# Linear attention and an MLP on one core: batch 1's loads moved to the software queue, chunks 1, 2 and 9 begun in token halves

## The chip, the core and the metric

The kernel runs on one NeuronCore of a Trainium2 chip. Five engines have instruction streams of their own: TensorE (PE, matmuls), VectorE (DVE), ScalarE (ACT), GpSimd (POOL) and SyncE (SP). Loads and stores are issued by SP (a hardware queue) or by GpSimd (the software queue), and move through the core's 16 DMA engines. The metric is device time in microseconds (us), the median of several executions.

## What is computed

The inputs are q, k, v of shape (8 batches, 8 heads, 576 tokens, 64), a gain g of 512, and two weights w1 (512 x 2048) and w2 (2048 x 512), all float32.

```python
q_s = softmax(q, axis=-1)                     # over the 64 of a head
k_s = softmax(k, axis=2)                      # over the 576 tokens
kv  = einsum('bhsd,bhse->bhde', k_s, v)
x   = einsum('bhsd,bhde->bhse', q_s, kv)      # then heads side by side: (8, 576, 512)
xn  = (x - mean(x)) / sqrt(var(x) + 1e-6) * g
out = x + relu(xn @ w_ch1) @ w_ch2
```

## The kernel before

Work is cut into nine chunks of 512 tokens. Chunks 0 to 7 hold the first 512 tokens of batches 0 to 7, and chunk 9 (`C9`, number 8 in the code) the 64 last tokens of all eight batches. Each chunk passes two stages. The attention stage takes exponentials of q and k (`exp_q`, `exp_k`, ACT), casts v to bfloat16 (`cast_v`, lines 146 to 152), multiplies k by v over all tokens (`kv_mm`, line 246, written to `pkv` and from there by VectorE into `kv_sb`), then q by that (`po_mm`, line 278), and normalises (`x_fast`, line 321: x, its mean and `xn`; `square_sum` and `rstd_op` on ACT give the deviation, which is applied only to the output). `xn` and the exponentials of q are transposed, for chunks 0 and 1 on PE (`pe_T`, line 775, with a copy by ACT or VectorE), later by DMA (`dma_T`, line 198). The 64 remaining tokens of k and v of a batch (`load_kvrem`, line 118, rows of 256 bytes) join through `prep_kvrem`.

The MLP stage multiplies `xn` by w1 into `ph` and takes the ReLU into `hT` (`mm1`, line 395: 64 matmuls of 128x512, 16 output blocks m of four k-steps each). For w2, chunk 0 uses plain matmuls (`mm2_stream`, line 456), which take w2's four row groups one after the other, for all four token tiles each. Chunks 1 and up use a Strassen-like scheme of seven half-size products (`mm2_fast`, line 584), in the order 1, 5, 6, 2, 7, 3, 4. It needs differences of w2 (`quarter_w2`, line 467; i is which difference, g the row half of w2) and sums of `hT` (`sum_h`, line 480, likewise). Product 5 reads sum 0, product 6 sum 1, product 7 sum 2, product 3 sum 3. Product 3 begins on a bank seeded by VectorE (`seed_e`).

In chunk 0, `mm1_part` (line 407) does w1's product in parts: a pair of output blocks shares a bank for one token half, and a part needs only the transposed tokens t0 to t0 + tn. Its ReLU is on VectorE for every second pair of the later token half.

The order is written out by hand. `run` (line 654) walks the matmuls of a chunk's MLP, each with a weight, and puts side work in when the sum of weights reaches a given position: a chunk's first product spans positions 0 to 64, and the second 64 to 128 in chunk 0, 64 to 120 in the others. The lines 940 to 970 give chunk 0's side work, which holds the attention stage of batch 1; `second_side` (line 736) gives chunk 1's, which holds that of batch 2. Every engine executes its own instructions in the order in which they are issued, and waits by semaphores.

The loads of the beginning, in order:

- SP: q of batch 0 (half), then k of batch 0 in four head pairs (line 823).
- GpSimd: v of batch 0; a small copy that reads the last head of k (line 844) and so waits for the fourth pair; w1's four column groups with q's second half after the first; w2's first two row groups (lines 845 to 850). These loads cast float32 to bfloat16.
- `load_gated(1, ...)` (line 894): for batch 1, GpSimd writes one element of each target when a weight has landed (line 899), and SP's load, which overwrites it, must wait for that. So q waits for w1's last group, k and v for w2's first.
- Line 925: GpSimd waits for the second half of batch 1's k; only then does it issue w2's third and fourth row group.
- `load_gated(2, ...)`: q of batch 2 waits for v of batch 1, k and v for w2's third group. Batches 3 and up are loaded by `load_batch` from SP.

The buffers `kt` and `vt` exist once, `qt` twice, so that batch 2's k waits until `exp_k(1)` has read batch 1's, and v until `cast_v(1)` has.

Of the kernel before, what the change touches and what calls it, by code (L numbers as in the profile page):

```python
# [20 lines left out]
def kernel(  # L21
# [384 lines left out]

    def mm1_part(c, m, t0, tn, ko):

        if "h" not in hbox:
            new_h()  # L410
        half, at = divmod(t0, 2)
        if m % 2 == 0 and at == 0 and ko == 0:
            hbox["ph", m // 2] = mm_ps.tile([P, 2, 2, P], FP32, tag="m", name="ph")
        ph = hbox["ph", m // 2]
        nc.tensor.matmul(  # L415
            ph[:, m % 2, at : at + tn], w1_sb[:, ko, m * P : (m + 1) * P],
            xnTs[c][:, t0 : t0 + tn, ko, :],
            start=(ko == 0), stop=(ko == KO1 - 1),
        )
        if m % 2 == 1 and at + tn == 2 and ko == KO1 - 1:  # L420
            dst = hbox["h"][:, m - 1 : m + 1, 2 * half : 2 * half + 2]
            if half and (m // 2) % 2 == 1:
                nc.vector.tensor_scalar_max(dst, in0=ph, scalar1=0.0)
            else:
                nc.scalar.activation(dst, ph, AF.Relu)
# [158 lines left out]
    def mm2_fast(c):  # L584

        steps = []

        def product(n, name, first=False, at=None, ts=range(2), own=False):
            at = at or {}
            for t in ts:  # L590
                for k in range(KH):
                    i = t * KH + k

                    def go(t=t, k=k, i=i):
                        if i == 0 and first:
                            bank(name)
                        prod(n, name, t, k, first or own, own)
                        for fn in at.get(i, []):
                            fn()

                    steps.append((0.5, go))

        def seed_c():
            bank("c")
            nc.scalar.copy(hbox["c"], hbox["a"])

        def seed_e():
            bank("e")
            add_u("e", "s2")

        if c == C9:
            last_products(product)
            return steps

        def ys(name, col, t0):
            return [lambda t=t: y_quarter(c, t0 + t, col, hbox[name][:, t]) for t in range(2)]

        product(1, "a", first=True, at={
            0: [lambda i=i: sum_h(1, i) for i in range(4)], 15: [seed_c]})
        product(5, "b", first=True)  # L620
        product(6, "a", at={15: [lambda: copy_u("s2")]})
        product(2, "c", at={7: [seed_e]})
        product(7, "a", at={2: ys("c", 0, 0)[:1], 5: ys("c", 0, 0)[1:], 15: [lambda: copy_u("s3")]})
        product(3, "e", at={13: [lambda: add_u("b", "s3")]})
        product(4, "a", at={
            1: ys("e", 1, 0)[:1], 4: ys("e", 1, 0)[1:],
            7: ys("b", 1, 2)[:1], 10: ys("b", 1, 2)[1:], 15: ys("a", 0, 2)})
        return steps

    def mlp_steps(c):  # L630
        full = range(KO2)
        first = []
        if c == 0:
            full = range(0)
            for n, t0, tn in ((0, 0, 1), (0, 1, 1), (1, 0, 2), (2, 0, 2), (3, 0, 2), (0, 2, 2), (1, 2, 2), (2, 2, 2), (3, 2, 2)):
                first += [
                    (0.25 * tn, lambda m=m, t0=t0, tn=tn, ko=ko: mm1_part(c, m, t0, tn, ko))
                    for m in range(4 * n, 4 * n + 4) for ko in range(KO1)
                ]
        first += [(1, lambda m=m, ko=ko: mm1(c, m, ko)) for m in full for ko in range(KO1)]  # L640
        if c == 0:
            return first + [
                (1, lambda t=t, ko=ko: mm2_stream(c, t, ko))
                for n in range(4) for t in range(T) for ko in range(4 * n, 4 * n + 4)
            ]
        if c >= FAST:
            return first + mm2_fast(c)
        return first + [(1, lambda t=t, ko=ko: mm2(c, t, ko)) for t in range(T) for ko in range(KO2)]
# [86 lines left out]

    def second_side():

        s = [(1 + 3 * i, lambda i=i: quarter_w2(i, 1)) for i in range(4)]
        s += [(15, lambda: square_sum(1, 3)), (30, lambda: rstd_op(1))]
        s += [(p, lambda w=w: load_batch(3, (w,))) for p, w in ((8, 2), (31, 0), (40, 1))]  # L740
        s += [(p + 11, fn) for p, fn in sums_fast(2)]
        s += [(12, lambda: exp_k(2, 0, 4)), (20, lambda: exp_k(2, 2, 4)), (25, lambda: prep_kvrem(2))]
        s += [
            (p, lambda j=j, e=e: cast_v(2, j, e))
            for p, j, e in ((31, 0, None), (31.4, 1, None), (31.8, 2, None), (32.2, 3, None))
        ]
        s += spread(
            [lambda j=j, t=t: kv_mm(2, j, t) for j in range(NP) for t in range(T + 1)], 35, 48
        )
        s += [(49, lambda: start_x(2))]  # L750
        for t, (p0, p1) in enumerate(((52, 58), (70, 77), (79, 84), (88, 93))):
            s += spread([lambda t=t, i=i: po_mm(2, t, i) for i in range(NP)], p0, p1)
            s += [(p1, lambda t=t: x_fast(2, t)), ((63, 84, 92, 105)[t], lambda t=t: square_sum(2, t))]
        s += [(78, lambda: xn_T(2, 0, 2)), (99, lambda: xn_T(2, 2, 2)), (106, lambda: rstd_op(2))]
        s += [(75, lambda: exp_q(3, 0, 4)), (79, lambda: exp_q(3, 2, 4)), (85, lambda: eq_T(3))]
        s += [(97, lambda: exp_k(3, 0, 4)), (108, lambda: exp_k(3, 2, 4)), (113, lambda: prep_kvrem(3))]
        s += [(p, lambda j=j: cast_v(3, j, nc.scalar)) for j, p in enumerate((101, 107, 111, 115))]
        return s
# [37 lines left out]
    def xn_pT(c, t, eng):  # L796
        pe_T(xnTs[c], xs[c][2][:, t], t, eng)

    def first_batch():
# [40 lines left out]
        for h0 in (0, 4):  # L840
            nc.gpsimd.dma_start(
                v0[0:P0, h0 : h0 + 4].rearrange("p h t d -> p h (t d)"), src0(v, h0, 4)
            )
        nc.gpsimd.tensor_copy(out=gate[0:P0], in_=k0[0:P0, H - 1, 0, 0:4])
        load_w1(0)
        load_q0(1, nc.gpsimd)
        for nb in range(1, 4):
# [43 lines left out]
        for i in range(NP):  # L891
            po_mm(0, t, i)

    def load_gated(b, src):

        alloc_batch(b)
        srcs = src if isinstance(src, tuple) else (src, src)
        for which in (2, 0, 1):
            nc.gpsimd.tensor_copy(out=raws[b][which][0:1, 0, 0, 0:1], in_=srcs[which < 2])
            if b == 1 and which == 0:  # L900
                load_main(nc.sync, b, which, 0, 4)
                load_main(nc.sync, b, which, 4, 4)
            else:
                load_main(nc.sync, b, which, 0, H)
            if which == 2:
                load_kvrem(nc.sync, b)

    def load_batch(b, parts=(2, 0, 1)):

# [9 lines left out]
    with tc.manual_schedule(  # L919
# [1 line left out]
                 mybir.EngineType.SP, mybir.EngineType.Pool}  # L921
    ):
        first_batch()
        load_gated(1, (w1_sb[0:1, 0, 1536:1537], w2_sb[0:1, 0, 0:1]))
        nc.gpsimd.tensor_copy(out=gate, in_=raws[1][0][:, 4, 0, 0:4])
        for g4 in range(2, 4):
            load_w2(g4)
        load_gated(2, (raws[1][1][0:1, 0, 0, 0:1], w2_sb[0:1, 8, 0:1]))
        def po_x(c, t):
            for i in range(NP):  # L930
                po_mm(c, t, i)
# [2 lines left out]
        def kv_all(c):  # L934
# [19 lines left out]
                (38, lambda: rstd_op(0)),  # L954
            ]
            + [(62, lambda: exp_q(1, 0, 4)), (64, lambda: exp_q(1, 2, 4))]
            + [(68 + t, lambda t=t: reduce_q(1, t)) for t in range(T)]
            + [(71.5, lambda: nc.vector.reciprocal(eqs[1][2], eqs[1][1]))]
            + [(72 + 4 * t, lambda t=t: eq_pT(1, t, (nc.scalar, nc.vector)[t % 2])) for t in range(T)]
            + [(80, lambda: prep_kvrem(1)), (82, lambda: exp_k(1, 0, 4)), (86, lambda: exp_k(1, 2, 4))]  # L960
            + [(p, lambda i=i: quarter_w2(i, 0)) for i, p in enumerate((61, 63, 65, 92))]
            + [(95 + 0.2 * j, lambda j=j: cast_v(1, j, (nc.vector, nc.vector, nc.scalar, nc.scalar)[j])) for j in range(NP)]
            + [(96, lambda: kv_all(1))]
            + [(96.5, lambda: (po_x(1, 0), po_x(1, 1)))]
            + [(100, lambda: po_x(1, 2)), (104, lambda: xn_pT(1, 0, nc.scalar)), (105, lambda: square_sum(1, 0))]
            + [(106, lambda: po_x(1, 3)), (112, lambda: xn_pT(1, 1, nc.scalar)), (113, lambda: square_sum(1, 1))]
            + [(118, lambda: xn_pT(1, 2, nc.scalar)), (119, lambda: square_sum(1, 2))]
            + [(126, lambda: xn_pT(1, 3, nc.scalar)), (122, lambda: exp_q(2, 0, 4)), (127, lambda: exp_q(2, 2, 4))]
            + [(127.8, lambda: eq_T(2))],
        )  # L970
        for c in range(1, B):
# [11 lines left out]
            if c == B - 2:  # L983
# [4 lines left out]
                    (96 + 10 * r, lambda r=r: nc.vector.reduce_sum(eqs[C9][1][:, r], eqs[C9][0][:, r], axis=AX.X))  # L988
                    for r in range(2)
                ]  # L990
            at = 49 if c == 1 else 33
            run(mlp_steps(c), side + [(at + (1 if c == 1 else 3) * i, lambda i=i: sum_h(0, i)) for i in range(4)])
        run(mlp_steps(C9), [(33 + 3 * i, lambda i=i: sum_h(0, i)) for i in range(4)])


# [28 lines left out]
```

## Time and profile before

| | |
|---|---|
| median of 13 executions | 289.15 us (288.46 to 290.5) |
| the profiled execution | 290.15 us, its span 288.4 us |
| PE busy | 270.4 us, 94% of the span |
| DVE, ACT, POOL busy | 197.0, 183.2, 28.1 us |
| granted PE clock | 1.00 in the windows up to 258 us, mean 0.999 |
| read from HBM, written | 36.70 MB, 9.44 MB |
| batch 0 to w1's product, chunk 0 | from 18.62 us |
| chunk 1's first matmul | 57.66 us |
| chunk 2's first matmul | 88.83 us |
| a steady chunk | 28.0 to 28.1 us |
| chunk 9's first matmul | about 258.1 us |

A row of a timeline gives start, length, engine, line, operation, output<-input, count and, in brackets, the idle time before and what ended it. A row of the waits gives who waited for whom: total, times, longest. A row of windows gives the stretch, its length, the busy time of PE, weight loads, DVE, ACT and POOL, the granted clock, the mean busy share of the DMA engines (which can exceed 1 where packets overlap) and GB/s. These count bytes at the target: a weight load of 1 MB in HBM counts half.

### The profile page before, as it was taken

To read this page: it belongs to the slowest core of one execution; us is meant where nothing else is said; L and a number is where in the kernel's file an instruction comes from. 1 tells how busy PE (TensorE), PEld (TensorE's weight loads), DVE (VectorE), ACT (ScalarE), POOL (GpSimd) and SP (SyncE) were. 2 spreads that over 40 slices of the span, in tenths; PEclk is the share of its full clock that TensorE was granted. 3 is DMA by queue.
4 is the path that set the end of the run, shared out by engine and by line. 5 is a ranking of instruction groups with operands and counts; after the bars stand their busy time and mean duration, and the time that the engine had idled before them with its cause. 6 is when DMAs were issued, how large, how long until landed. Compare 5 with 4: busy or idle time off the path is not lost.

```text
span 288.4 us, 5282 instructions
## 1 busy us (share of the span) xinstructions
PE 270.4 (94%) x2058; PEld 183.0 (63%) x2058; DVE 197.0 (68%) x451; ACT 183.2 (64%) x343; POOL 28.1 (10%) x58
## 2 busy tenths in 40 slices
PE   7769997897999999999999999999999999999994
PEld 2558845444685568647854785488548845874583
DVE  3746486964898567885787577768676939871463
ACT  3545763796777778487947884877586378526500
POOL 2520020200002000200020011001100200020000
PEclk9999999999999999999999999999999999999999
DMA  7999999998978985698769858984923520132014
GB/s 182 162 234 206 257 270 183 263 330 248 282 89 244 332 146 106 210 343 110 109 211 367 95 99 278 330 84 95 251 38 41 142 94 3 36 96 88 0 39 109
DMA packets 73627, 49.04 MB, mean 170 GB/s; under 512 B 42241, under 2 KB 71425, under 8 KB 73602
## 3 DMA queue, kind: packets, MB, share of 16 engines
q1 hardware_dynamic: 65282, 34.48, 52.8%
q0 software_dynamic: 7728, 13.70, 19.8%
q10 hardware_dynamic: 592, 0.52, 0.5%
q8 instruction: 16, 0.26, 0.4%
q14 instruction: 9, 0.07, 0.1%
HBM read 36.70 MB, written 9.44 MB: 160 GB/s over the span
## 4 chain that ended last, share of the span: by engine, by line
PE 63%; DMA 17%; DVE 8%; SPq 5%; ACT 2%; POOL 1%; issue 1%; POOLq 0%; DVEq 0%; ACTq 0%
PE ph L400 32%; PE ba L507 16%; DMA vt<-in_v_dram 9%; DMA w_sb<-in_moe_w_ch_dram 4%; PE be L507 4%; PE bc L507 4%; PE bb L507 4%; DVE hs L491 4%; DMA kt<-in_k_dram 3%; SPq L121 2%; PE pkv L246 2%; SPq L113 2%; DVE x L294 2%; PE po L278 2%; DMA xnT<-xn 1%
## 5 line engine op out<-in xcount | busy, mean ns | idle before, releaser
L400 PE MATMUL ph<-xnT,w_sb 128*128 128x512 bf16 x512 | 123.0, 379 | 1.9 <-ACT xnT L780 1.4
L388 ACT ACTIVATE hT<-ph 128x512 bf16<-128x512 f32 x128 | 74.5, 596 | 42.3 <-PE ph L400 42.1
L400 PEld LDWEIGHTS <-w_sb 128*128 128x128 bf16 x512 | 48.0, 98 | 54.5 <-issue 4.2
L507 PEld LDWEIGHTS <-hs 128*128 128x128 bf16 x512 | 49.1, 98 | 7.4 <-DVE hs L491 1.0
L491 DVE TENSOR_TENSOR hs<-hT 128x1024 bf16<-128x1024 bf16 x32 | 22.0, 688 | 28.4 <-ACT hT L388 28.2
L507 PEld LDWEIGHTS <-hT 128*128 128x128 bf16 x384 | 36.7, 98 | 5.2
L524 POOL DMA_DIRECT2D out_dram<-ot x28 | 15.1, 542 | 187.0 <-DVE ot L518 186.7
L507 PE MATMUL ba<-w_q,hs 128*128 128x256 bf16 x256 | 31.3, 273 | 0.6 <-ACT s L532 0.6
L317 DVE SCALAR_TENSOR_TENSOR xn<-x,mv,g_bc 128x512 bf16<-128x512 bf16 x34 | 25.6, 752 | 1.2
L311 ACT ACTIVATE junk<-x,mv 128x512 bf16<-128x512 bf16 x34 | 24.6, 722 | 2.5 <-DVE mv L330 2.3
L324 DVE SCALAR_TENSOR_TENSOR x<-po,rq 128x512 bf16<-128x512 f32 x30 | 20.6, 687 | 7.1 <-PE po L278 6.8
L278 PE MATMUL po<-kv_sb,eqT 128*128 128x128 bf16 x128 | 23.9, 219 | 0.6 <-DVE kv_sb L255 0.6
L246 PE MATMUL pkv<-vm,ek 128*128 128x129 bf16 x112 | 21.7, 220 | 1.6 <-DVE vm L152 1.6
L532 ACT COPY s<-ba 128x512 f32<-128x512 f32 x15 | 8.8, 585 | 14.0 <-PE ba L507 13.7
L278 PEld LDWEIGHTS <-eqT 128*128 128x128 bf16 x128 | 11.5, 98 | 9.3 <-DVE kv_sb L255 1.8
L460 PE MATMUL pc<-w_sb,hT 128*128 128x512 bf16 x64 | 15.9, 379 | 1.5 <-DMA w_sb<-in_moe_w_ch_dram 1.5
L415 PE MATMUL ph<-xnT,w_sb 128*128 128x256 bf16 (+1 forms) x144 | 15.4, 261 | 1.5 <-ACT xnT L780 1.2
L507 PE MATMUL bb<-w_q,hs 128*128 128x256 bf16 x128 | 16.0, 273 | 0.5 <-DVE hs L491 0.5
L719 DVE TENSOR_REDUCE zq<-eq 128x8 f32<-128x512 bf16 x26 | 16.3, 694 | 0.0
L175 ACT ACTIVATE eq<-qt 128x1024 bf16<-128x1024 f32 x14 | 14.6, 1055 | 2.6 <-DMA qt<-in_q_dram 2.6
L507 PE MATMUL ba<-w_sb,hT 128*128 128x256 bf16 x128 | 16.1, 273 | 0.0
L507 PE MATMUL bc<-w_sb,hT 128*128 128x256 bf16 x128 | 15.7, 273 | 0.0
(118 smaller groups left out, 317.4 us busy)
## 6 DMA issues: line engine op xcount, KB each, us to landing
out_dram<-ot POOLq DMA_DIRECT2D x32, 256.0 KB, 3.0
qt<-in_q_dram SPq DMA_DIRECT2D x7, 1024.0 KB, 10.7
vt<-in_v_dram SPq DMA_DIRECT2D x7, 1024.0 KB, 12.7
kt<-in_k_dram SPq DMA_DIRECT2D x6, 1024.0 KB, 10.1
w_sb<-in_moe_w_ch_dram POOLq DMA_DIRECT2D x8, 512.0 KB, 10.4
kt<-in_k_dram SPq DMA_DIRECT2D x4, 288.0 KB, 6.6
kt<-in_k_dram SPq DMA_DIRECT2D x2, 512.0 KB, 9.0
qr<-in_q_dram SPq DMA_DIRECT2D x8, 128.0 KB, 4.7
```

The lines of the kernel that those rows point to most:

```text
L246: nc.tensor.matmul(pkv[:, j % 2, 0:w], lhsT, rhs, start=(t == 0), stop=(t == last))
L278: nc.tensor.matmul(pobox["p"][:, i * P : i * P + P], eqTs[c][:, t, i, :], kv_sb[:, c, i, :], start=True, stop=True,)
L311: nc.scalar.activation(junk, x[:, t], AF.Square, bias=mv[:, t, 0:1], accum_out=mv[:, t, 1:2])
L317: nc.vector.scalar_tensor_tensor(xn[:, t], in0=x[:, t], scalar=mv[:, t, 0:1], in1=g_bc, op0=ALU.add, op1=ALU.mult)
L324: nc.vector.scalar_tensor_tensor(x[:, t].rearrange("p (h d) -> p h d", h=H), in0=pobox[c, t].rearrange("p (h d) -> p h d", h=H), scalar=1. ...
L388: nc.scalar.activation(dst, src, AF.Relu)
L400: nc.tensor.matmul(hbox["ph"], w1_sb[:, ko, m * P : (m + 1) * P], xnTs[c][:, :, ko, :], start=(ko == 0), stop=(ko == KO1 - 1),)
L415: nc.tensor.matmul(ph[:, m % 2, at : at + tn], w1_sb[:, ko, m * P : (m + 1) * P], xnTs[c][:, t0 : t0 + tn, ko, :], start=(ko == 0), stop=( ...
L460: nc.tensor.matmul(hbox["pc", t], hbox["h"][:, ko, t, :], w2_sb[:, ko, :], start=(ko == 0), stop=(ko == KO2 - 1),)
L491: nc.vector.tensor_tensor(out=dst, in0=x, in1=y, op=op)
L507: nc.tensor.matmul(hbox[bank][:, t], lhsT, rhs, start=first and (own or t == 0) and k == 0, stop=k == KH - 1, skip_group_check=True)
L719: s = spread([lambda t=t: nc.vector.reduce_sum(zq[:, t], eq[:, t], axis=AX.X) for t in range(T)][t0:], 0, 12)
```

## The change

The diff does five things.

1. The gate ahead of w1 reads head 5 of k instead of head 7: it waits for the third pair of heads.
2. `load_second` replaces `load_gated(1)`: q, k, v of batch 1 and the remainders are issued by GpSimd with no gate, directly behind w2's second group, and w2's third and fourth group directly behind them. `load_third` replaces `load_gated(2)`: GpSimd waits for v of batch 1, issues v of batch 2 itself, and SP issues q, k and the remainders.
3. Chunks 1, 2 and 9 do the first four output blocks by `mm1_part` in token halves (0, 1) and (2, 3), with ReLUs on ACT alone; the rest as before.
4. In chunk 1 (`FAST`), only one sum of the first half is made before the second product; the others are interleaved with the sums of the second half in three places.
5. Side work is moved: `quarter_w2` of the first half earlier and of the second half partly later, the casts of batch 1's v all on VectorE, the transposed copies of its q all on ACT, its remainders prepared last, square sums of chunk 1 later, and the attention stage of batch 2 a few positions earlier.

```diff
     def mm1_part(c, m, t0, tn, ko):
 
-        if "h" not in hbox:
+        if (m, t0, ko) == (0, 0, 0):
             new_h()
...
-            if half and (m // 2) % 2 == 1:
+            if c == 0 and half and (m // 2) % 2 == 1:
...
+        def sums(*which):
+            return [lambda g=g, i=i: sum_h(g, i) for g, i in which if g or c == FAST]
+
+        late = c == FAST
         product(1, "a", first=True, at={
-            0: [lambda i=i: sum_h(1, i) for i in range(4)], 15: [seed_c]})
-        product(5, "b", first=True)
-        product(6, "a", at={15: [lambda: copy_u("s2")]})
+            0: sums((1, 0), (0, 1), (1, 1)) + ([] if late else sums((1, 2), (1, 3))), 15: [seed_c]})
+        product(5, "b", first=True, at={8: sums((0, 2), (1, 2)) if late else []})
+        product(6, "a", at={8: sums((0, 3), (1, 3)) if late else [], 15: [lambda: copy_u("s2")]})
...
+        elif c in (1, 2, C9):
+            full, parts = range(4, KO2), ((0, 0, 2), (0, 2, 2))
...
-        s = [(1 + 3 * i, lambda i=i: quarter_w2(i, 1)) for i in range(4)]
-        s += [(15, lambda: square_sum(1, 3)), (30, lambda: rstd_op(1))]
+        s = [(p, lambda i=i: quarter_w2(i, 1)) for i, p in enumerate((1, 4, 44, 46))]
+        s += [(42, lambda: square_sum(1, 2)), (46, lambda: square_sum(1, 3)), (54, lambda: rstd_op(1))]
...
-        s += [(12, lambda: exp_k(2, 0, 4)), (20, lambda: exp_k(2, 2, 4)), (25, lambda: prep_kvrem(2))]
+        s += [(12, lambda: exp_k(2, 0, 4)), (17, lambda: exp_k(2, 2, 4)), (23, lambda: prep_kvrem(2))]
...
-        for t, (p0, p1) in enumerate(((52, 58), (70, 77), (79, 84), (88, 93))):
+        for t, (p0, p1) in enumerate(((51, 56), (66, 73), (76, 81), (87, 93))):
...
-        nc.gpsimd.tensor_copy(out=gate[0:P0], in_=k0[0:P0, H - 1, 0, 0:4])
+        nc.gpsimd.tensor_copy(out=gate[0:P0], in_=k0[0:P0, 5, 0, 0:4])
...
-    def load_gated(b, src):
...
+    def load_second():
+
+        alloc_batch(1)
         for which in (2, 0, 1):
...
+            load_main(nc.gpsimd, 1, which, 0, H)
+        load_kvrem(nc.gpsimd, 1)
+
+    def load_third():
+
+        alloc_batch(2)
+        nc.gpsimd.tensor_copy(out=raws[2][2][0:1, 0, 0, 0:1], in_=raws[1][1][0:1, 0, 0, 0:1])
+        load_main(nc.gpsimd, 2, 1, 0, H)
+        for which in (2, 0):
+            load_main(nc.sync, 2, which, 0, H)
+        load_kvrem(nc.sync, 2)
...
-        load_gated(1, (w1_sb[0:1, 0, 1536:1537], w2_sb[0:1, 0, 0:1]))
-        nc.gpsimd.tensor_copy(out=gate, in_=raws[1][0][:, 4, 0, 0:4])
-        for g4 in range(2, 4):
-            load_w2(g4)
-        load_gated(2, (raws[1][1][0:1, 0, 0, 0:1], w2_sb[0:1, 8, 0:1]))
+        load_second()
+        load_w2(2)
+        load_w2(3)
+        load_third()
...
-            + [(68 + t, lambda t=t: reduce_q(1, t)) for t in range(T)]
-            + [(71.5, lambda: nc.vector.reciprocal(eqs[1][2], eqs[1][1]))]
-            + [(72 + 4 * t, lambda t=t: eq_pT(1, t, (nc.scalar, nc.vector)[t % 2])) for t in range(T)]
-            + [(80, lambda: prep_kvrem(1)), (82, lambda: exp_k(1, 0, 4)), (86, lambda: exp_k(1, 2, 4))]
-            + [(p, lambda i=i: quarter_w2(i, 0)) for i, p in enumerate((61, 63, 65, 92))]
-            + [(95 + 0.2 * j, lambda j=j: cast_v(1, j, (nc.vector, nc.vector, nc.scalar, nc.scalar)[j])) for j in range(NP)]
+            + [(67 + t, lambda t=t: reduce_q(1, t)) for t in range(T)]
+            + [((72, 76, 86, 90)[t], lambda t=t: eq_pT(1, t, nc.scalar)) for t in range(T)]
+            + [(78, lambda: nc.vector.reciprocal(eqs[1][2], eqs[1][1]))]
+            + [(80, lambda: exp_k(1, 0, 4)), (84, lambda: exp_k(1, 2, 4))]
+            + [(94 + 0.2 * j, lambda j=j: cast_v(1, j)) for j in range(NP)]
+            + [(p, lambda i=i: quarter_w2(i, 0)) for i, p in enumerate((55, 58, 60, 62))]
+            + [(95.9, lambda: prep_kvrem(1))]
...
-            + [(118, lambda: xn_pT(1, 2, nc.scalar)), (119, lambda: square_sum(1, 2))]
-            + [(126, lambda: xn_pT(1, 3, nc.scalar)), (122, lambda: exp_q(2, 0, 4)), (127, lambda: exp_q(2, 2, 4))]
+            + [(118, lambda: xn_pT(1, 2, nc.scalar))]
+            + [(126, lambda: xn_pT(1, 3, nc.scalar)), (119, lambda: exp_q(2, 0, 4)), (127, lambda: exp_q(2, 2, 4))]
...
-            at = 49 if c == 1 else 33
-            run(mlp_steps(c), side + [(at + (1 if c == 1 else 3) * i, lambda i=i: sum_h(0, i)) for i in range(4)])
+            sums = [(57, 0)] if c == FAST else [(33 + 3 * i, i) for i in range(4)]
+            run(mlp_steps(c), side + [(at, lambda i=i: sum_h(0, i)) for at, i in sums])
```

More of the change, by code (lines that the diff above doesn't have):

```diff
@@ L631, in mlp_steps @@
         full = range(KO2)
-        first = []
+        first, parts = [], ()
         if c == 0:
             full = range(0)
[L635 to L639, printed above, removed]
+            parts = ((0, 0, 1), (0, 1, 1), (1, 0, 2), (2, 0, 2), (3, 0, 2), (0, 2, 2), (1, 2, 2), (2, 2, 2), (3, 2, 2))
+        elif c in (1, 2, C9):
+            full, parts = range(4, KO2), ((0, 0, 2), (0, 2, 2))
+        for n, t0, tn in parts:
+            first += [
+                (0.25 * tn, lambda m=m, t0=t0, tn=tn, ko=ko: mm1_part(c, m, t0, tn, ko))
+                for m in range(4 * n, 4 * n + 4) for ko in range(KO1)
+            ]
         first += [(1, lambda m=m, ko=ko: mm1(c, m, ko)) for m in full for ko in range(KO1)]
@@ L750, in second_side @@
         s += [(49, lambda: start_x(2))]
-        for t, (p0, p1) in enumerate(((52, 58), (70, 77), (79, 84), (88, 93))):
+        for t, (p0, p1) in enumerate(((51, 56), (66, 73), (76, 81), (87, 93))):
             s += spread([lambda t=t, i=i: po_mm(2, t, i) for i in range(NP)], p0, p1)
-            s += [(p1, lambda t=t: x_fast(2, t)), ((63, 84, 92, 105)[t], lambda t=t: square_sum(2, t))]
-        s += [(78, lambda: xn_T(2, 0, 2)), (99, lambda: xn_T(2, 2, 2)), (106, lambda: rstd_op(2))]
+            s += [(p1, lambda t=t: x_fast(2, t)), ((63, 82, 92, 105)[t], lambda t=t: square_sum(2, t))]
+        s += [(78, lambda: xn_T(2, 0, 2)), (98, lambda: xn_T(2, 2, 2)), (106, lambda: rstd_op(2))]
         s += [(75, lambda: exp_q(3, 0, 4)), (79, lambda: exp_q(3, 2, 4)), (85, lambda: eq_T(3))]
@@ L892, in q0_rest @@
             po_mm(0, t, i)
-    def load_gated(b, src):
-        alloc_batch(b)
-        srcs = src if isinstance(src, tuple) else (src, src)
+    def load_second():
+        alloc_batch(1)
         for which in (2, 0, 1):
[L899 to L906, printed above, removed]
+            load_main(nc.gpsimd, 1, which, 0, H)
[7 more added lines that the diff above has]
+        load_kvrem(nc.sync, 2)
     def load_batch(b, parts=(2, 0, 1)):
```

## The prediction

> **What bounds the kernel now.** I read the busy row of the 40 slices first, then the waits of PE, then the timelines of PE, GpSimd (POOL) and ACT around those waits, then one-microsecond windows of the DMA share.
>
> ```profile
> PE   7769997897999999999999999999999999999994
> ...
> 89.00:117.20 28.20, 28.20 (x214) 19.34 (x213) 20.32 (x50) 21.50 (x40) 2.14 (x4) 1.00 0.77 189
> ...
> 145.20:173.30 28.10, 28.10 (x214) 19.27 (x213) 20.61 (x50) 20.27 (x38) 2.19 (x5) 1.00 0.81 198
> ```
>
> The two windows (length, then busy time of PE, weight loads, DVE, ACT, POOL; granted clock; DMA share; GB/s) are whole chunks of the steady part. PE is busy for all of their length at full clock. From 89 us on nothing can be gained but a shift: whatever the front loses less, the end comes earlier. The front's stalls, from the waits of PE between 18 and 89 us:
>
> ```profile
> PE pkv L246 <- DVE vm L152: 1.6, 1, 1.6
> PE pc L460 <- DMA w_sb<-in_moe_w_ch_dram: 1.5, 1, 1.5
> PE ph L400 <- ACT xnT L780: 1.4, 1, 1.4
> PE ph L415 <- ACT xnT L780: 1.2, 2, 0.7
> PE ptr L778 <- ACT eq L175: 0.7, 1, 0.7
> PE ph L400 <- DMA xnT<-xn: 0.5, 1, 0.5
> PE bb L507 <- DVE hs L491: 0.5, 1, 0.5
> PE ph L415 <- DMA w_sb<-in_moe_w_ch_dram: 0.4, 1, 0.4
> ```
>
> In order of time they are 0.38 at 26.67 (w1's last quarter), 0.66 at 38.37 (q of batch 1), 1.48 at 47.14 (w2's third quarter), 1.37 at 57.66 (start of chunk 1), 1.57 at 66.95 (v of batch 2), 0.49 at 77.57 (a sum) and 0.55 at 88.83 (start of chunk 2): 6.5 us. The loads behind the middle ones, from the timelines of POOL and ACT, two windows of 3 us, and the chain of waits (start, length, what):
>
> ```profile
> 40.67 0.19 POOL L925 COPY gate<-kt 128x4 f32<-128x4 f32 x1 [11.19 <-DMA kt<-in_k_dram]
> 41.12 1.50 POOL L95 DMA_DIRECT2D w_sb<-in_moe_w_ch_dram  x2 [0.26 <-issue]
> ...
> 56.08 1.06 ACT L175 ACTIVATE eq<-qt 128x1024 bf16<-128x1024 f32 x1 [0.84 <-DMA qt<-in_q_dram]
> ...
> 38.00:41.00 3.00, 2.63 (x20) 1.55 (x21) 2.62 (x5) 1.04 (x3) 0.19 (x1) 1.00 1.10 348
> 41.00:44.00 3.00, 3.00 (x19) 1.48 (x17) 2.72 (x7) 2.95 (x4) 1.91 (x3) 1.00 0.70 151
> ...
> 3.12 7.47 DMA kt<-in_k_dram
> 14.32 12.31 DMA w_sb<-in_moe_w_ch_dram
> 34.24 9.13 DMA vt<-in_v_dram
> 50.86 15.52 DMA vt<-in_v_dram
> ```
>
> w2's later half is not even issued before 41.12, because GpSimd waits for k. Around each such gate the DMA share falls from about 1.2 to 0.6-0.9 (11 to 14 us, 41 to 44, 46 to 48): holes worth some 3 us of transfer. v of batch 2 lands at 66.38 and is the last link before PE runs free.
>
> **w1 begun at k's third pair.** The fourth pair landed at 10.59, and the gate ran at 10.71. The four landings took 6.0, 6.6 and 7.5 us (least, median, most); ACT's wait shows 6.2 for the second, so the median makes the third 7.0, landed at 9.63. w1 is issued 1.0 us earlier. Its first bytes now come near 14, after a hole; at 13 they would still miss the fourth pair, so chunk 0's start (18.62) stays. The queue moves up by 1.0: w1 complete 25.7, w2's first quarters 28.2 and 30.7 (2.54 each: 26.63 to 29.17 in the gates now). The 0.38 goes.
>
> **Batch 1 in the software queue.** The casting weights move 1 MB of source in 2.54 us, a batch load of 1.05 MB at 348 GB/s (38 to 41 us) in 3.0. So q, k, v of batch 1 land at 33.7, 36.7, 39.7; now k lands at 40.6, v at 43.4. Of the 0.66 some 0.3 stays: ACT reaches the exponential at about 35.4 in any case and needs 2.0 us. The remainders of k and v (0.26 MB in 256-byte rows) have no row on this queue. On SP's queue they show as the low stretch at 77 to 79 (200, 90 GB/s) or 34 to 36 (180): 1.5 to 2.3 us. I take 1.9.
>
> [...] The row: w1's and w2's six issues from 11.2 to 16.6 took 0.75 to 0.79 each, q's half 0.92, with DVE busy more than half the time. By the row, the five batch loads and two w2 quarters cost about 6.1 us of GpSimd, done at 22.7, before the data of the first is due (30.7). [...] I take the row.
>
> **w2's third and fourth quarter.** GpSimd runs past them at once, so it then waits for v of batch 1 (39.7), marks q of batch 2, and SP issues q, then k once `exp_k(1)` is done near 41. Nothing is queued behind GpSimd's wait but v of batch 2 and, from 55, the outputs. From 41 on SP's transfers share the engines. The share has a row: w2's fourth quarter came about 5.0 after the third (PE took it at 52.2 after 47.14) against 2.54 alone, so half. Left at 41: 0.6 of remainders and 2.54, doubled: the third quarter lands near 47.2, the fourth at 52.1. Bounds: 44.0 with no sharing, 48.5 with slow remainders. **So this part wins nothing at 47.14**; what was won earlier is waited away there, and earlier than 46.1 PE could not use it, as the second product of that place needs `kv_sb`, whose chain (pkv to VectorE) takes 1.2 us after the last pkv matmul.
>
> **Start of chunk 1.** ACT no longer waits for q of batch 2 before its last transposed copy: issued at 40.3, it took 12.0 us when issued at 43.96, so 52 at worst, and the exponential is due at about 53.5. Besides, chunk 1 now begins with 32 half-width matmuls (3.5 us) that need only tokens already there. PE goes on where chunk 0's last matmuls end now (55.69 + 0.59 = 56.3) instead of at 57.66: 1.4 won. If w2 is early or late this becomes 2.8 (the `kv_sb` limit) or 0.2.
>
> **v of batch 2.** It stands in the software queue behind w2, and its buffer is free when the casts of batch 1, all on VectorE now, end near 41.5. At half share it takes 52.1 to 58; PE needs it at 56.3 + 6.8 = 63. The 1.57 goes, with 5 us to spare. k of batch 2 (exponential at about 58.8) lands between 47 and 57.
>
> **Sums of chunk 1.** The 0.49 is a chain: four sums at 71.91 hold `x_fast`, that holds ACT's square sum, that holds the last ReLU at 76.30. Three of them move behind; the 0.49 goes. Price: eight sums (5.0), four `x_fast` (6.3), two adds (1.3) and the eight output quarters (3.5) now share the last 15 us of the chunk on VectorE. Up to the seed of the third product I count 10.3 us of VectorE work in 11.0 us of PE time. Taken at nothing; if that cover is gone, PE waits there by what is late.
>
> **Halves.** Chunks 1, 2 and 9 replace 16 matmuls of 0.2158 by 32 of 0.1092: +0.04 each, +0.12 in all. In chunk 2 the 0.55 goes, since the second transpose gains 3.5 us of cover; in chunk 9 PE has no wait (its 64 follow at 258.10 without a gap), so the halves bring nothing. w2's moved differences, the square sums, the ReLUs now on ACT alone in these chunks: ACT is busy 14 of 16 us in chunk 1's first product by count, covered by six banks.
>
> **Sum:** 1.4 + 1.57 + 0.49 + 0.55 - 0.12 = 3.9. The profiled execution has a span of 288.4 and took 290.15; it becomes 284.5 and 286.25. It lies 1.0 above the median of 289.15; on the median the forecast is **285.2**.
>
> **Rivals.**
> 1. *w2 comes early* (SP's q takes little of the engines): third quarter by 46, chunk 1 starts at 54.9. For: between 44 and 46 the rate, 188 GB/s, is nearly that of weights alone (206). Against: the 5.0 above. Gain 5.3: 283.9. Chance 0.22.
> 2. *VectorE piles up in chunk 1*: the sums hold the seed and the next chunk's banks; 1 us at the seed and 1 at chunk 2. For: DVE is at 4.3 to 4.8 of 5 from 75 to 90 us today. Against: it now idles for 2 us before 66. The gain falls from 3.9 to 1.9: 287.2. Chance 0.15.
> 3. *w2 comes late, slower than before*: the 256-byte remainders stand in order ahead of w2; at 5 us or more for them, or with starved descriptors, w2's third quarter lands near 52.5 and its fourth at 57. PE waits at the place of today's 1.48; each us past 47.2 costs one. It decides from a landing of 51.1 on. Time: 290.5. For: no remainder has run on this queue. Against: the half q did, in 512-byte rows, at 338 and 288 GB/s. Chance 0.15.
> 4. *Nothing moves* because transfers stay saturated whatever their order: against it the three holes; 289.1, chance 0.05.
>
> My forecast has 0.43. A difference under 0.2% (0.6 us) cannot be told from none here. Faster: 0.43 + 0.22 + 0.15 = 0.80, of which I give 0.02 away to late starts nobody counted: 0.78. Same 0.05, slower 0.17. The range is from 283.2 (all stalls gone, no price) to 289.0: it leaves out the slower case alone. The likeliest case's own range is 284.3 to 286.8.
>
> **What would show it.** w2's third quarter landing near 47 with PE waiting 2 us or more there; no wait at the start of chunks 1 and 2; pkv of chunk 2 without a wait; v of batch 2 landing before 60; the steady chunks still 28.0 to 28.1. Wrong if GpSimd's issues stretch beyond 1 us each, if w2 lands past 49, or if a wait for `be` or `hs` appears in chunk 1.

## The result, and the profile after

| | before | after |
|---|---|---|
| median in the comparison | 288.91 us (287.68 to 290.5, 48 executions) | 284.37 us (282.91 to 287.11, 11 executions) |
| ratio, 95% interval | 1 | 0.9851 (0.983 to 0.9873) |
| profiled execution, its span | 290.15, 288.4 us | 283.91, 282.1 us |
| chunk 0's w1 product begins | 18.62 us | 17.73 us |
| chunk 1 begins | 57.66 us | 53.81 us |
| chunk 2 begins | 88.83 us | 81.92 us |
| chunk 9 begins | 258.10 us | 251.69 us |

The kernel is 4.5 us faster on the medians, and 6.24 us in the two profiled executions. The difference of starts splits the 6.3 us of span: 0.89 before chunk 0's first product, 2.96 from there to chunk 1, 3.06 within chunk 1, and 0.61 given back after chunk 2's start. The 0.89 is no effect of the change. The first half of q of batch 0, whose load no edit touches, landed at 6.19 in the profile of before, at 5.30 in that of after, and between 4.97 and 5.67 in the twelve experiments. In e11 below, which has the loads of before, chunk 0 begins at 17.79. So the profiled execution of before was late there by chance, which may be most of its 1.2 us above its median. The other shares are those of one execution of each kernel: e11 has 37.83 from chunk 0 to 1 and 30.72 for chunk 1, where before has 39.04 and 31.17, so each share can be off by about 1 us.

PE's busy row on the page of after, then two steady chunks in the windows (columns as before):

```profile
PE   8879998999999999999999999999999999999993
```

```profile
110.20:138.30 28.10, 28.10 (x213) 19.25 (x212) 20.78 (x50) 20.58 (x38) 2.18 (x5) 1.00 0.82 197
138.30:166.30 28.00, 28.00 (x213) 19.25 (x212) 20.57 (x49) 20.26 (x38) 2.08 (x5) 1.00 0.86 198
```

The steady chunks are what they were, 28.0 to 28.1 us, so the gain is a shift made in the front. The waits of PE after; the rows left out lie before 20 us, ahead of chunk 0's product or at its start:

```profile
PE po L278 <- DVE kv_sb L255: 1.1, 2, 0.6
...
PE pkv L246 <- DVE vr L158: 0.7, 1, 0.7
PE ba L507 <- ACT s L532: 0.6, 1, 0.6
PE ph L400 <- DMA xnT<-xn: 0.3, 1, 0.3
```

Of the seven stalls of before, none is left: `w_sb`, the exponential of q, `vm`, `hs` and the two starts of chunks are gone from the list. (The wait for `s` was there before as well, and so was the first of the two for `kv_sb`, 0.61 at 14.51, in batch 0's attention. The one of 0.3 is at the start of chunk 6.) Two others have come at the hinge between chunk 0's second product and batch 1's attention, as PE's timeline shows:

```profile
43.15 0.22 PE L246 MATMUL pkv<-vr,ekr 128*128 128x129 bf16 x1 [0.75 <-DVE vr L158]
...
45.37 0.49 PE L278 MATMUL po<-kv_sb,eqT 128*128 128x128 bf16 x6 [0.53 <-DVE kv_sb L255]
```

PE now waits for the remainders of v, and then for `kv_sb`, which is what stood behind w2 in the prediction. Chunk 1's first 32 half-width matmuls follow at 53.81 without a wait. GpSimd's timeline gives the new order of the loads (lines 113 and 121 are batch 1, line 95 is w2):

```profile
15.94 0.89 POOL L113 DMA_DIRECT2D kt<-in_k_dram  x1 [0.27 <-DMA w_sb<-in_moe_w_ch_dram]
...
20.32 0.69 POOL L121 DMA_DIRECT2D ktr<-in_k_dram  x1 [1.56 <-DMA w_sb<-in_moe_w_ch_dram]
22.92 0.69 POOL L121 DMA_DIRECT2D vtr<-in_v_dram  x1 [1.91 <-DMA w_sb<-in_moe_w_ch_dram]
25.44 0.77 POOL L95 DMA_DIRECT2D w_sb<-in_moe_w_ch_dram  x1 [1.83 <-DMA w_sb<-in_moe_w_ch_dram]
27.95 0.75 POOL L95 DMA_DIRECT2D w_sb<-in_moe_w_ch_dram  x1 [1.73 <-DMA w_sb<-in_moe_w_ch_dram]
41.31 0.37 POOL L911 COPY qt<-vt 1x1 f32<-1x1 f32 x1 [12.61 <-DMA vt<-in_v_dram]
```

Each issue took 0.69 to 0.96 us, as in the trace of before; but from k on GpSimd waits between them (the row of v, left out, shows 1.04). w2's last group is issued at 27.95, not at 41.12 and later as before.

### The profile page after: what moved, and what is told of

Read it like the earlier page. It is cut to its first block, busy times and chain, and to the rows that moved or that the text cites. A ratio compares the mean times of both kernels' runs of the same rounds, so it can differ in the third digit from the quotient of the medians.

```text
span 282.1 us, 5365 instructions
## 1 busy us (share of the span) xinstructions
PE 270.7 (96%) x2106; PEld 188.0 (67%) x2106; DVE 196.5 (70%) x451; ACT 181.9 (64%) x343; POOL 32.2 (11%) x58
## 4 chain that ended last, share of the span: by engine, by line
PE 76%; DMA 11%; DVE 8%; ACT 3%; issue 1%; DVEq 0%; ACTq 0%
PE ph L400 33%; PE ba L507 17%; DMA vt<-in_v_dram 8%; PE be L507 4%; PE bb L507 4%; PE ph L415 4%; PE bc L507 4%; PE pkv L246 3%; PE po L278 2%; PE pc L460 2%; DVE hs L491 2%; DVE x L294 2%; DMA qt<-in_q_dram 2%; DMA xnT<-xn 1%; DVE kv_sb L255 1%
## 5 line engine op out<-in xcount | busy, mean ns | idle before, releaser
L400 PE MATMUL ph<-xnT,w_sb 128*128 128x512 bf16 x464 | 111.7, 379 | 0.3 <-DMA xnT<-xn 0.3
L388 ACT ACTIVATE hT<-ph 128x512 bf16<-128x512 f32 x116 | 66.6, 598 | 32.9 <-PE ph L400 32.8
L400 PEld LDWEIGHTS <-w_sb 128*128 128x128 bf16 x464 | 43.3, 98 | 45.5 <-DMA xnT<-xn 0.6
L491 DVE TENSOR_TENSOR hs<-hT 128x1024 bf16<-128x1024 bf16 x32 | 21.9, 688 | 28.7 <-ACT hT L388 28.5
L507 PEld LDWEIGHTS <-hT 128*128 128x128 bf16 x384 | 36.7, 98 | 5.2
L415 PE MATMUL ph<-xnT,w_sb 128*128 128x256 bf16 (+1 forms) x240 | 27.2, 265 | 1.0 <-ACT xnT L787 0.9
L415 PEld LDWEIGHTS <-w_sb 128*128 128x128 bf16 x240 | 21.6, 98 | 3.7 <-issue 1.1
L425 ACT ACTIVATE hT<-ph 128x512 bf16<-128x512 f32 x24 | 13.8, 596 | 9.1 <-PE ph L415 9.1
```

What stands on the lines that cost most here:

```text
L388: nc.scalar.activation(dst, src, AF.Relu)
L400: nc.tensor.matmul(hbox["ph"], w1_sb[:, ko, m * P : (m + 1) * P], xnTs[c][:, :, ko, :], start=(ko == 0), stop=(ko == KO1 - 1),)
L415: nc.tensor.matmul(ph[:, m % 2, at : at + tn], w1_sb[:, ko, m * P : (m + 1) * P], xnTs[c][:, t0 : t0 + tn, ko, :], start=(ko == 0), stop=( ...
L491: nc.vector.tensor_tensor(out=dst, in0=x, in1=y, op=op)
L507: nc.tensor.matmul(hbox[bank][:, t], lhsT, rhs, start=first and (own or t == 0) and k == 0, stop=k == KH - 1, skip_group_check=True)
```

## The experiments

In each profile I read the times at which chunks 0, 1 and 2 begin, since part of the executions has a slow stretch of PE's clock before 24 us (last section) that moves everything behind it, and shortens the stretch from chunk 0 to 1 (in e1, e3, e4, e6 and e9). The length of chunk 1 is free of that. The stretch lifts medians as well. A long one, by the measure of the last section, is in three of six executions of e1, e2 and e3 and in two of six of e4 and e6, but only in 3 of 17 of the changed kernel (those of after and e9), whose other 14 have a median of 283.9. So I also give the medians without these executions.

| kernel | median us (n) | ratio to before, 95% | chunk 0 to 1 | chunk 1's length |
|---|---|---|---|---|
| before | 288.91 (48) | 1 | 39.04 | 31.17 |
| after | 284.37 (11) | 0.9851 (0.983-0.9873) | 36.08 | 28.11 |
| e1: no halves | 286.16 (6) | 0.9904 (0.9866-0.9942) | 36.85 | 29.14 |
| e2: no halves in chunk 1 | 285.81 (6) | 0.9867 (0.983-0.9905) | 36.26 | 28.06 |
| e3: sums as before | 286.47 (6) | 0.9909 (0.9875-0.9943) | 36.54 | 28.92 |
| e4: w1 after the fourth pair | 285.57 (6) | 0.9882 (0.9853-0.9911) | 35.49 | 28.11 |
| e5: all but the loads | 287.19 (22) | 0.9947 (0.9928-0.9965) | 37.28 | 30.52 |
| e6: the loads alone | 286.95 (6) | 0.9933 (0.9908-0.9957) | 36.38 | 29.48 |
| e7: remainders last | 291.28 (1) | - | 41.95 | 28.10 |
| e8: remainders first | 284.99 (4) | 0.9865 (0.9841-0.989) | 36.53 | 28.11 |
| e9: after, again | 283.91 (5) | 0.9831 (0.98-0.9861) | 34.99 | 28.11 |
| e10: after, PE kept busy | 283.05 (4) | 0.9799 (0.9771-0.9826) | 35.70 | 28.11 |
| e11: before, PE kept busy | 288.44 (22) | 0.9979 (0.9962-0.9995) | 37.83 | 30.72 |
| e12: e10, one cast on ACT | 283.34 (4) | 0.9801 (0.9775-0.9827) | 35.28 | 28.11 |

**e1, the halves.** From the changed kernel, in `mlp_steps`:

```diff
-        elif c in (1, 2, C9):
-            full, parts = range(4, KO2), ((0, 0, 2), (0, 2, 2))
```

> The changed kernel with chunks 1, 2 and 9 at full width again. Theory (each half gives cover to a late transposed piece): ACT still waits for batch 2's q until 53.4 us, so chunk 1 starts about 1.0 later, and chunk 2's second transpose, issued at about 79.9 with 4.0 to land, comes some 1.8 late; 0.12 comes back. Time 287.0 (286.3 to 287.5). Rival (the halves bring nothing, the loads do it all): 284.3.

PE's timeline of e1:

```profile
57.23 7.71 PE L400 MATMUL ph<-xnT,w_sb 128*128 128x512 bf16 x35 [0.88 <-ACT xnT L785]
...
86.37 0.60 PE L400 MATMUL ph<-xnT,w_sb 128*128 128x512 bf16 x2 [0.91 <-DMA xnT<-xn]
```

Both waits that the halves were to cover are back, 0.88 for the last transposed copy and 0.91 for the second transpose: 1.8 us in all. The medians differ by 1.8 too, but without the long slow stretches by 1.5 (285.4 of three executions against 283.9), and the two intervals touch, so that the equality is partly luck. The theory holds for the cause; at chunk 2 it counted twice what came.

**e2, the halves in chunk 1 alone.** `elif c in (2, C9):` in place of `(1, 2, C9)`.

> The changed kernel with chunk 1 alone at full width. Theory: only the wait at chunk 1's start returns, +1.0 - 0.04; chunk 2 keeps its cover: 285.3. Rival (the halves matter at chunk 2 only): 284.4. If both waits of the first run hang on one another, this run is as slow as that one.

In the timeline of PE the wait stands at chunk 1's start as expected, 1.11 us:

```profile
53.80 7.71 PE L400 MATMUL ph<-xnT,w_sb 128*128 128x512 bf16 x35 [1.11 <-ACT xnT L787]
```

Yet its chunk 1 starts where that of after does. PE would without the wait have been there 1.1 us earlier than after was, because in this execution v of batch 1 was there at 39.78, 1.4 sooner. The median is 1.4 us above that of after with overlapping intervals, but that is the slow stretch: the three executions without a long one have a median of 283.92, just that of the changed kernel. So the wait is shown, and a gain of time from the halves of chunk 1 is not; the rival, that they matter at chunk 2 only, stays open.

**e3, the sums.** `late = False`, and chunk 1's four sums of the first half at positions 49 to 52 again.

> The changed kernel with the four first-half sums of chunk 1 at positions 49 to 52 again and the second half's all at the first step of product 1. Theory: the sums hold x_fast, that holds ACT's square sum and the last ReLU, product 5 waits some 0.5 us: 284.9. Rival (the later placing crowds VectorE and costs as much as it wins): 284.4 or less.

```profile
73.48 0.61 PE L507 MATMUL bb<-w_q,hs 128*128 128x256 bf16 x4 [0.63 <-DVE hs L491]
```

This row of PE's timeline is the 0.49 of before, come back as 0.63 where after has none, and chunk 1 is 0.81 longer. The median is 2.1 us above that of after, and 1.9 without the three executions that have a long slow stretch (285.8 against 283.9). The trace accounts for 0.8 of it, so about 1 us isn't explained; a short slow stretch, which the profiled execution had (granted clock 0.57 from 16 to 20 us), may be part of it.

**e4, w1's start.** The gate reads head `H - 1` again.

> The changed kernel with the gate ahead of w1 on k's fourth pair again. Theory (the software queue is one stream, so 1.0 us at its head moves every landing): v of batch 1 lands near 42.2, the wait for its casts grows by 0.9, w1's last quarter makes PE wait 0.4 again (part of the same time): 285.3. Rival (the hole is refilled by what stands behind, nothing moves): 284.4.

It is 1.2 us above after in the medians, and 1.15 without the slow stretches, near the theory's 1.0, though the two intervals overlap. Its profile fell into the slow clock (mean 0.980) and can't be read for this.

**e5 and e6, the two halves of the change.** e5 is the changed kernel with `load_gated` and line 925's gate in their old places; it keeps w1's early gate. e6 is the kernel before with nothing changed but w1's gate and the loads. So w1's early gate is in both. The cut shows e6's loads:

```diff
-        load_second()
-        load_w2(2)
-        load_w2(3)
-        load_third()
+        load_gated(1, (w1_sb[0:1, 0, 1536:1537], w2_sb[0:1, 0, 0:1]))
+        nc.gpsimd.tensor_copy(out=gate, in_=raws[1][0][:, 4, 0, 0:4])
+        for g4 in range(2, 4):
+            load_w2(g4)
+        load_gated(2, (raws[1][1][0:1, 0, 0, 0:1], w2_sb[0:1, 8, 0:1]))
```

> The changed kernel with the gated loads of before (batch 1 from SP behind gates, w2's later half behind k, batch 2 all from SP); w1's early gate, halves, sums and positions stay. Theory (the order of the loads is the larger part): w2's third group makes PE wait about 1.3 again, v of batch 2 lands near 65.5 while PE is ready for it near 62.5, so 3 us more: 284.4 + 4.0 = 288.4. Rival (the schedule of the side work is the larger part): 285.5.

> The kernel before with the loads alone changed (w1's gate, batch 1 and w2 in the software queue, v of batch 2 behind them). Theory: the waits for w2, for batch 2's q at chunk 1's start and for its v go, those inside chunk 1 and at chunk 2 stay; ACT now waits for the remainders ahead of k's exponentials, which eats what was won at w2: gain 2.5 to 3.2, time 286.0. Rival (the loads alone bring all of it): 284.5.

In e5, PE's timeline shows v of batch 2 worse than before (1.57 there):

```profile
64.89 0.22 PE L246 MATMUL pkv<-vm,ek 128*128 128x129 bf16 x1 [2.25 <-DVE vm L152]
```

PE comes for it 2.7 us earlier than before (62.64 against 65.38), and the wait for its cast ends only 2.1 earlier (64.89 against 66.95), so the wait grows. In e6 that wait is gone, and those that have nothing to do with loads remain, in the same view:

```profile
74.53 0.50 PE L507 MATMUL bb<-w_q,hs 128*128 128x256 bf16 x3 [0.49 <-DVE hs L491]
85.83 0.60 PE L400 MATMUL ph<-xnT,w_sb 128*128 128x512 bf16 x2 [0.58 <-DMA xnT<-xn]
```

Against the runs of before beside them, the loads alone bring some 2.0 us (0.67%), the rest alone 1.5 to 1.7 (0.53%); together they bring 4.5 (1.49%). The whole is more than the two parts, although w1's gate counts in both; but with intervals of 0.2% each the difference of 0.3% is not clear of noise. What the traces show is that each part alone runs into waits that the other removes.

**e7 and e8, where the remainders stand.** e7 issues them behind w2's fourth group; e8 ahead of q, with their preparation at position 79 and two of v's casts on ACT.

```diff
-        load_kvrem(nc.gpsimd, 1)
...
         load_w2(2)
         load_w2(3)
+        load_kvrem(nc.gpsimd, 1)
```

> The changed kernel with the remainders of batch 1 behind w2's fourth group. It asks why v lands at 41.2 although the rate of its stream falls at 37.5. Theory A (some engines lag, the queue is in order): v lands at 41 as before. Theory B (the 256-byte rows behind it hold its completion up): v lands near 39. In both the remainders land near 44.5 and PE waits for them, 2 us more in all: about 286.5.

> The changed kernel with batch 1's remainders ahead of its q, prepared at position 79, and v's casts two on VectorE and two on ACT. Theory A: v lands 1.6 later (42.8), the shorter casts win 1.1 back: 284.9. Theory B: v lands near 40.7, casts end near 41.6 and the wait of 0.75 goes: 283.7, better than both kernels.

PE's timeline of e7, then of e8:

```profile
47.90 0.27 PE L246 MATMUL pkv<-vr,ekr 128*128 128x129 bf16 x1 [4.69 <-DVE vr L158]
```

```profile
36.43 0.28 PE L785 MATMUL ptr<-ident,eq 128*128 128x128 bf16 x2 [0.34 <-ACT eq L175]
37.38 0.28 PE L785 MATMUL ptr<-ident,eq 128*128 128x128 bf16 x2 [0.66 <-ACT eq L175]
45.80 0.49 PE L278 MATMUL po<-kv_sb,eqT 128*128 128x128 bf16 x6 [0.54 <-DVE kv_sb L255]
```

Behind w2 the remainders of k were in use at 46.56 only, PE stood 4.69 us for them, and one execution took 291.28: dearer by nearly 5 us than either theory had said. One part is that the remainders came later than the 44.5 expected, probably because by then they share the engines with SP's loads of batch 2, which this run doesn't separate. Another is PE's clock, the third column from the end, in the windows of e7:

```profile
45.00:46.00 1.00, 0.00 (x0) 0.00 (x0) 0.00 (x0) 0.00 (x0) 0.00 (x0) 0.61 1.16 278
...
51.00:52.00 1.00, 0.78 (x6) 0.57 (x5) 0.85 (x3) 0.00 (x0) 0.00 (x0) 0.50 1.02 336
52.00:53.00 1.00, 1.00 (x9) 0.56 (x8) 0.99 (x2) 0.00 (x0) 0.00 (x0) 0.98 1.09 348
```

In the long stand the clock fell to half, from 45.2 to 52.0. From the end of the stand to chunk 1 PE took 11.8 us (47.90 to 59.69), where after took 10.7 for the same work (43.15 to 53.81). v landed at 40.17 in e7, between the two theories' times, and decides nothing between them. Ahead of q they cost q: 1.0 us of PE at 36 to 38, the prepared remainders then wait for nobody, but v still lands at 41.15 (41.21 in after), and PE's wait for `kv_sb` is as in after. By the traces the place chosen by the change is the best of the three; by the times it is better than e7, while the interval of e8 overlaps that of after.

**e9 to e12, the idle places of PE.** e10 adds 17 matmuls of 128x256 on data nobody reads, in three places ahead of chunk 0's first product where PE waits anyway; e11 does the same to the kernel before; e12 also moves the last of v's four casts to ACT. e9 is the changed kernel once more, beside them.

```diff
-            warm(4)
+            warm(4 if t else 10)
...
+        warm(6)
         for t in range(2):
             for i in range(NP):
                 po_mm(0, t, i)
...
+        warm(5)
         xn_pT(0, 0, nc.scalar)
```

> The changed kernel once more, as the control of this series. The runs so far show executions in which PE's clock is granted at half for 3 to 10 us between 8 and 24 us (mean 0.98). Theory (the front of the changed kernel is bound by PE there, that of the kernel before by its loads): 284.0 at a mean clock of 0.99 and up, 287 below, and the kernel before equal in both (289). Rival (the clock dip costs every kernel the same): 2 us in both.

> The changed kernel with 17 more dummy matmuls (128x256) in three idle places of PE between 8 and 18 us. Theory (the half clock follows from idle time ahead of it): fewer or no executions below 0.988, median 284.0, none at 287. Rival (the dip does not depend on these gaps): as many as in the control, same median.

> The kernel before with the same 17 dummy matmuls. Theory (the loads hide the clock there): no gain, 289 (288.5 to 289.5). Rival (the early clock costs it too): 1 us faster.

> The changed kernel with the dummy matmuls and the last of v's four casts on ACT, behind the exponential of the remainders. Theory (PE's 0.75 wait is casts and then the remainders' cast in a row on VectorE): 0.4 us shorter there, 283.6. Rival (the landing of the remainders binds, not the casts): as without.

e10 has the lowest median: 283.05 us, 0.9799 of before, and all four executions at a mean clock of 0.997 or more; its interval overlaps that of e9 beside it. The same matmuls bring the kernel before 0.2% (0.9979), 0.6 us in the medians, between the theory's nothing and the rival's 1; what it comes from stays open. e12 reaches chunk 1 in 35.28 us instead of 35.70, but has a new wait of 0.79 us for a ReLU at 98.38 in chunk 2 and no better time; e9, without the moved cast, has 0.19 us at that place, so the cast is not its only cause, and how much it adds one trace can't say. The theory of e12, that the casts and the remainders' cast in a row make PE wait, fits its trace (0.20 for `vr` in e10, none in e12), but not by a shorter time.

## Why the prediction was right, and the term that was off

The forecast of 285.2 us was 0.8 above the 284.37 measured, inside the likeliest case's own range. Its direction held, and so did its terms for the sums, the halves and v of batch 2. What failed is the term for w2's third quarter: it came some 3 us earlier than forecast, so what came at this place is rival 1, for which the prediction had 283.9. That is also where the executions without a long slow stretch lie (283.9). That the median stands nearer to the forecast is partly luck: the slow stretches lift it, and a price behind chunk 2 was not counted. Of the signs named, PE's wait of 2 us for w2 near 47 did not come; the other signs of being right came, and none of being wrong.

- **w1 begun early.** Seen in GpSimd's waits: they end at 25.44 and 27.95, when w1's fourth group and w2's first land, if each waits for the load eight ahead of it (forecast 25.7 and 28.2). The 0.38 is gone; e4 puts the whole step at about 1, not clear of noise.
- **Batch 1's q, k, v.** q and k landed in time for exponentials at 33.99 and 37.94 without a wait (forecast landings 33.7, 36.7), so the 0.3 that was to remain of the 0.66 is gone too. v landed at 41.2, not 39.7, and made the 0.75 of PE shown above. That is one draw: with the same loads VectorE began its casts of v at 39.78 in e2, 40.43 in e12 and 40.67 in e10, and in e3 PE's wait for the remainders behind v ended at 44.41, against 43.15 in after. The 0.53 for `kv_sb` is not v's: it is 0.48 in e2 and 0.54 in e9, where PE did not wait for v at all. It belongs to the chain from the last pkv matmul over VectorE, which the prediction had as its limit of 1.2 us (44.22 to 45.37 here).
- **GpSimd's issues.** The prediction took the row of before (0.75 to 0.92 an issue). The row was right: the seven issues took 0.69 to 0.96 each and 5.6 us together, against 6.1 counted. They ended at 28.7 rather than 22.7 because of the waits between them; nothing was late for it, as v's data wasn't through before 41.
- **w2's third quarter: the term that was mis-sized.** The prediction halved its rate from 41 us on, when SP issues q of batch 2, and had it land at 47.2: "So this part wins nothing at 47.14", and 1.4 at chunk 1. The halving was read from the 5.0 us between two rows of PE in before:

```profile
47.14 0.38 PE L460 MATMUL pc<-w_sb,hT 128*128 128x512 bf16 x1 [1.48 <-DMA w_sb<-in_moe_w_ch_dram]
...
52.22 1.46 PE L460 MATMUL pc<-w_sb,hT 128*128 128x512 bf16 x6
```

  The second is no landing. PE reached the fourth quarter there without a wait, and the sixteen matmuls of the third with the side work among them take PE about as long in any case: 5.56 us in after (44.35 to 49.91), with the 0.53 for `kv_sb` in it. So the trace of before held no row for the share. In the windows of after:

```profile
38.00:41.00 3.00, 3.00 (x22) 1.59 (x20) 0.84 (x2) 2.50 (x5) 0.00 (x0) 1.00 1.18 160
41.00:44.00 3.00, 2.25 (x25) 1.58 (x24) 2.13 (x7) 1.14 (x2) 1.17 (x2) 1.00 1.24 208
44.00:47.00 3.00, 2.34 (x22) 1.32 (x20) 2.48 (x9) 0.00 (x0) 0.10 (x1) 1.00 1.13 338
```

  From 38 to 41 the last columns show the 256-byte remainders, 160 GB/s at full share. From 41 to 44 they show 208 GB/s at full share, the rate of casting weights alone (203 to 204 from 16 to 28 us): q, issued at 41.71, moved next to nothing before 44. So the third quarter was through by about 44, the bound "with no sharing". After has no wait for it to measure, and took it at 44.35; where the matmul came sooner it did wait, until 43.12 in e2, 43.95 in e10 and 43.66 in e12, each time about 3.3 us behind the first cast of v. Why q moved so late stays open. Chunk 1 then began 2.96 us earlier relative to chunk 0, not 1.4; that is rival 1's mechanism, and near its 2.8. The two executions overstate it: 1.37 of it is the wait at chunk 1's start, which was only 0.43 in e11 with the loads of before.
- **q of batch 2** was given "52 at worst". The timeline of ACT:

```profile
53.36 1.06 ACT L175 ACTIVATE eq<-qt 128x1024 bf16<-128x1024 f32 x1 [1.15 <-DMA qt<-in_q_dram]
```

  Issued at 41.71 instead of 40.3, it took 11.6 us and was 1.15 late. PE did not notice, because of the halves; e1 and e2 show what it pays without them (0.88, 1.11).
- **v of batch 2.** Issued at 43.20, 1.7 later than counted: the issue waited for VectorE's casts of batch 1, that of v's remainders last. Its cast at 59.73 waited for no load, and PE came for it at 61.40 without a wait (7.6 us behind the start of chunk 1, where the prediction reckoned 6.8). The 1.57 is gone, as e6 shows by itself.
- **Sums and halves.** The 0.49 and the 0.55 are gone, and return in e3 (0.63) and e1 (0.91). VectorE ended the seed at 78.25, PE began the third product at 78.42: the cover counted as 10.3 in 11.0 us was 0.2 us wide, and rival 2 was a near thing. Chunk 1 became 3.06 us shorter; the terms within it summed to 2.6.
- **After chunk 2** the sum had 0.1 us of price; 0.6 was paid, 0.3 of it the wait at chunk 6, which e5 (0.28) and e8 (0.37) also have, e6 and e9 not; its cause stays open. In all, by these two executions: +1.5 at chunk 1's start, +0.5 in chunk 1, -0.5 later, which with the chance 0.89 makes the 6.3 us of span where the sum had 3.9.
- **Rival 3**, w2 late behind the remainders, did not come: they held the queue for the 2 us counted. No run shows the starved descriptors that it also names; none of the seven issues took more than 0.96 us. e7 shows that its danger was real in another place: it is the remainders that must not come late.

## What to carry to other kernels

When loads stand in one queue that lands them in the order of issue, as the software queue did here (in after q by 33.99, k by 37.94, v at 41.2, w2's third group by 44.35), lay them out by their rates from the trace, and let a second queue share only from the time at which its data is seen to move, not from its issue. Before a landing is read from the engine that uses the data, see that this engine waited: the start of a matmul that waits for nothing shows the engine's pace and not the transfer's. A load that is moved earlier pays in full only if the other waits of that stage go with it: here the loads alone and the rearranged work alone brought 2 us or less each, and each met the waits that the other takes away. Where a join needs a big load and a small one, the small one stood best directly behind the big one here: ahead of the queue it cost PE 1.0 us, at its end 4.7.

## What the runs showed of the hardware

**Eight loads under way.** GpSimd stood 1.6 to 1.9 us before four of its issues, each time until a weight had landed, 2.5 us apart like w1's and w2's groups. Counted back, each waits for the load eight earlier on that queue. It was free here. The number is counted and was not tested.

**A landing trails its data.** In after, v's stream gives way to the low-rate remainders at about 38 us (291 GB/s from 37 to 38, 141 from 38 to 39), yet VectorE begins on v at 41.2; in e2 the rate falls in the same microsecond (214) and VectorE begins at 39.78. In e7, with nothing small behind v, the two are 37 to 38 (270) and 40.17, so these runs do not show that small rows hold a landing up.

**PE's clock fell in part of the executions.** The windows of after, then of e4, from 12 to 20 us; the third column from the end is the granted clock, and (x..) after PE's busy time the number of matmuls:

```profile
12.00:16.00 4.00, 2.61 (x37) 2.15 (x35) 2.44 (x8) 0.69 (x2) 3.73 (x6) 1.00 1.15 254
16.00:20.00 4.00, 3.10 (x46) 2.77 (x45) 1.18 (x2) 2.27 (x5) 1.72 (x2) 1.00 1.22 203
```

```profile
12.00:16.00 4.00, 3.53 (x33) 3.31 (x32) 1.32 (x5) 0.00 (x0) 4.00 (x6) 0.50 1.05 216
16.00:20.00 4.00, 2.73 (x16) 1.80 (x15) 2.29 (x4) 1.15 (x3) 2.28 (x3) 0.50 1.19 217
```

At half clock chunk 0's product begins at 20.18 in e4 and 20.38 in e1, some 2.5 us late. Added up from the granted shares, the stretch lasted about 10.2 us in e1, e4 (which also has 0.88 from 8 to 12 us and 0.84 from 20 to 24) and e6, and 3.4 in e3 and e9; the mean clock of these executions is 0.979 to 0.982 and 0.991. So a mean below 0.988 shows a long stretch, and one near 0.991 can hide a short one. Three of 17 executions of the changed kernel had a long one, with 285.27, 286.99 and 287.11 us against a median of 283.9 of the others; 20 of 65 of the kernel before, with 288.53 against 289.30 of the others, so there it cost nothing. e5, with the gated loads, had 287.18 with it (3) and 287.22 without (19). I read this so, and did not test it further: with gated loads PE next waits for them, and the lost time goes into those waits; the changed kernel has taken them away, and so has become open to it.

In these stretches the windows show half the clock (0.50), for 3.4, 6.8 (e7) and 10.2 us, near one, two and three times the shortest. What starts and what ends a stretch the traces do not settle: in e4 the clock fell at 11.0, and until then PE had not stood longer than 1.2 us at a time; in e7 it fell at 45.2, when PE had stood for 2.0 us (since 43.20). With the 17 extra matmuls none of 30 executions (e10, e11, e12) had a long stretch. For the kernel before that is well supported, 0 of 22 in e11 against 6 of the 27 beside them and 20 of all 65, though three of the 22 have a mean of 0.992 or 0.993; for the changed kernel the eight executions are too few against 3 of 17.
